# A layer norm and two matmuls on one core: the first three token tiles are transposed raw and corrected later

## The chip, the cores and the metric

The kernel runs on one core of one Trainium2 chip. The metric is the device time in microseconds of one launch. The core has five engines with instruction streams of their own, which wait for one another through semaphores: PE (TensorE, matmuls and transposes into PSUM), DVE (VectorE), ACT (ScalarE), POOL (GpSimd) and SP (SyncE, which here only issues DMA transfers).

## The reference

```python
def _layernorm(x, axis=-1, eps=1e-5):
    m = jnp.mean(x, axis=axis, keepdims=True)
    v = jnp.var(x, axis=axis, keepdims=True)
    return (x - m) / jnp.sqrt(v + eps)

# x (1, 2048, 1024), w1 (1024, 3584), b1 (3584), w2 (3584, 1024), b2 (1024), all bf16
def reference(x, w1, b1, w2, b2):
    y = _layernorm(x, axis=-1)
    h = _gelu(jnp.einsum("bsd,df->bsf", y, w1) + b1)     # tanh form
    return jnp.einsum("bsf,fd->bsd", h, w2) + b2
```

## The kernel before

The 2048 tokens are 16 tiles of 128, in four blocks of four tiles. The first matmul needs y with the contraction on the partitions, so each tile of x is normalised in its own layout and then transposed into `yT_sb` (two buffers, one block each, 8 contraction slices of 128). The first product runs over 28 rows (128 columns of w1 each). One row of one block is a PSUM bank: eight products of 128x128 weights with 512 columns. ACT evaluates GELU with b1 from PSUM into `hT_sb` (`act_gelu`, L430). The second product (`out_chunk`, L453) makes 128x512 pieces of the output with 28 products each; DVE adds b2 and SP stores them. PSUM has `ps_t` (one bank, for transposes at first and then a row), `ps_1` (five) and `ps_2` (two).

The program is written out as one list per engine, in order. Each operation names the events that it waits for and the event that it signals; `_emit` (L71) turns them into semaphore waits. An engine's order is therefore the order of the calls that built its list. Only DVE's list is partly planned: `crit` and `fill` are merged by estimated due times (L569 to L584).

The start is done differently from the rest. While the weights of the first seven rows arrive in eight chunks of one contraction slice each (`w0` to `w7`, 896 columns), block 0 is worked as a wave: 224 products of 128 columns for seven rows at a time, tile by tile and slice by slice (L505 to L534), into seven open banks. Transposes of block 0 are PE transposes (`pe_T`, L367) with a copy by ACT; from block 1 on, DVE transposes 32x32 blocks (`ops_T`, L344).

Tile 0 is centred with a mean that DVE and ACT take together (L274, L494), tile 1 with its mean alone (L286); their deviations are spread over the partitions later (`ops_rbc`, L326) and multiplied onto columns 0 to 255 of every row of block 0 in PSUM (`dve_scale`, L423). Tiles 2 and 3 are normalised in full before their transposes. The power -1/2 of the variance is POOL's (L268). Until the first tile is ready PE runs products of ones (`warm`, L488): 34, then 3, then 3.

After the wave, `mm1_rows` (L536) goes on with rows 7 to 27 of block 0, the first of them in bank `ps_t`, the next in the banks of rows 0 to 4 as their GELUs end.

Of the kernel before, what the change touches and what calls it, by code (L numbers as in the profile page):

```python
# [11 lines left out]
P = 128  # L12
# [3 lines left out]
K_GROUPS = 2  # L16
# [4 lines left out]
WARM_A = ((34, None), (3, "m4"))  # L21
WARM_B = 3
N_CENTRED = 2
T_PUTS = {0: (None, None, 6), 1: (21, 35), 2: (96, 118), 3: (140, 156)}
NORM = {0: (0, 2, 8), 1: (0, 4, 8), 2: (0, 4, 8)}
GROUPS_0 = (0, 2, 5, 8)
WAVE_ROWS_0 = 6
WAVE_K = (0, 2, 4, 5, 6, 8)
GROUPS_1 = (0, 4, 8)
W1_CHUNK_COLS = (512, 512, 1024, 640)  # L30
N_W2_CHUNKS = 4
SP_FIRST_LOADS = ("x0a", "w0", "w1", "w2", "w3", "w4", "w5", "x2a", "x2b", "w6", "w7", "x3a", "x3b", "b1", "w8")
ACT_FIRST_LOADS = ("x0b", "x1")

T_PE_START = 5.7
T_DVE_START = 16.5
# [54 lines left out]
def bass_standalone__mixer_channel_mlp__prompt_kernel(  # L91
# [22 lines left out]
    nkg = max(1, min(K_GROUPS, DT))  # L114
    KGROUPS = [(h * DT // nkg, (h + 1) * DT // nkg) for h in range(nkg)]
    assert NB1 + NB2 + 1 <= 8 and NB2 == 2
    assert all(c[-1] == DT for c in (*NORM.values(), GROUPS_0, GROUPS_1, WAVE_K))
# [27 lines left out]
    with ExitStack() as es:  # L145
# [19 lines left out]
        half_sb = sb("half_sb", [P, 1], F32)  # L165
        m4_sb = sb("m4_sb", [P, 1], F32)
        rq_sb = sb("rq_sb", [P, N_CENTRED, 32], F32)
        rbc_sb = sb("rbc_sb", [P, N_CENTRED, P], F32)

# [4 lines left out]
        ps_tf = ps_t[:, :, :].bitcast(F32)  # L174

# [37 lines left out]
        def issue(item):  # L213
            if item[0] == "x" and item[-1] in "ab":
# [44 lines left out]
        pool.op(lambda e: e.memset(b1r_sb[:, :], 0.0), sig="b1z")  # L259
        dve.op(lambda e: e.memset(st_sb[:, :, 12:14], 0.0))  # L260
# [6 lines left out]
        def op_aggr(i):  # L267
            pool.op(lambda e, i=i: e.tensor_tensor(out=rstd_sb[:, i:i + 1], in0=mv_sb[:, i, 1:2],  # L268
                                                   in1=nhalf[:, i:i + 1], op=ALU.pow),
                    waits=[f"mv{i}", "nhalf"], sig=f"rstd{i}")  # L270
            return (lambda e, i=i: e.bn_aggr(mv_sb[:, i, :], st_sb[:, i, :]),  # L271
                    [f"st{i}_0", f"st{i}_1", "eps"], f"mv{i}", 0.33)

        def op_mean0():  # L274
            return (lambda e: e.tensor_scalar(out=m4_sb[:, :], in0=st_sb[:, 0, 1:2], scalar1=st_sb[:, 0, 4:5],
                                              scalar2=half_sb[:, :], op0=ALU.add, op1=ALU.add),
                    ["st0_0", "half"], "m4", 0.1)

        def op_norm(i, c0, c1, sig):
            if i == 0:  # L280
                return (lambda e, c0=c0, c1=c1: e.tensor_scalar(
                            out=o_sb[:, 0, c0:c1], in0=x_sb[:, 0, c0:c1], scalar1=4.0,
                            scalar2=m4_sb[:, :], op0=ALU.mult, op1=ALU.subtract),
                        ["m4"], sig, 0.02 + (c1 - c0) * 0.00055)
            if i < N_CENTRED:
                return (lambda e, i=i, c0=c0, c1=c1: e.tensor_scalar(  # L286
                            out=x_sb[:, i, c0:c1], in0=x_sb[:, i, c0:c1], scalar1=mv_sb[:, i, 0:1],
                            scalar2=None, op0=ALU.subtract),
                        [f"mv{i}"], sig, 0.02 + (c1 - c0) * 0.00055)
            return (lambda e, i=i, c0=c0, c1=c1: e.tensor_scalar(  # L290
                        out=x_sb[:, i, c0:c1], in0=x_sb[:, i, c0:c1], scalar1=mv_sb[:, i, 0:1],
                        scalar2=rstd_sb[:, i:i + 1], op0=ALU.subtract, op1=ALU.mult),
                    [f"rstd{i}", f"mv{i}"], sig, 0.02 + (c1 - c0) * 0.00055)
# [3 lines left out]
        def ops_norm(i):  # L297
            cuts = NORM.get(i, (0, DT))
# [27 lines left out]
        def ops_rbc():  # L326
            res = []
            for i in range(N_CENTRED):
                res.append((lambda e, i=i: e.tensor_scalar(out=rq_sb[:, i, :], in0=ones[:, 0:32],
                                                           scalar1=rstd_sb[:, i:i + 1], scalar2=(1.0 if i else 0.25),  # L330
                                                           op0=ALU.mult, op1=ALU.mult),
                            ["ones", f"rstd{i}"], f"rq{i}", 0.1))
            for tq in range(4):
                for q in range(4):
                    src = rq_sb[32 * tq:32 * (tq + 1), :, :]
                    dst = rbc_sb[32 * q:32 * (q + 1), :, 32 * tq:32 * (tq + 1)]
                    res.append((lambda e, src=src, dst=dst: e.transpose(out=dst, in_=src), [f"rq{N_CENTRED - 1}"],  # L337
                                ("rbc" if tq == 3 and q == 3 else None), 0.1))
            return res
# [4 lines left out]
        def ops_T(i):  # L344
            blk, t = divmod(i, TPB)
            waits = [y_ev[i][-1]]
            if blk - 2 in mm1_done:
                waits.append(mm1_done[blk - 2])
            res = []
# [15 lines left out]
        t_banks = [("t", ps_t[:, 0, :]), ("2_0", ps_2b[:, 0, :]), ("t", ps_t[:, 0, :])]  # L365

        def pe_T(i, groups, k):  # L367
            blk, t = divmod(i, TPB)
            j0, j1 = groups[k], groups[k + 1]
            bname, bap = t_banks[k if i == 0 else 0]  # L370
            evs = yT_ev.setdefault(i, [None] * DT)
            for j in range(j0, j1):
                waits = []
                if j == j0:
                    waits = ["ident"] + ([bank_read[bname]] if bname in bank_read else [])
                if j == j0 or y_ev[i][j] != y_ev[i][j - 1]:
                    waits.append(y_ev[i][j])
                pe.op(lambda e, i=i, j=j, o=(j - j0) * P, bap=bap: e.transpose(  # L378
                    out=bap[:, o:o + P], in_=(x_sb[:, i] if i else o_sb[:, 0])[:, j * P:(j + 1) * P],
                    identity=ident[:, :]),  # L380
                    waits=waits, sig=(f"tp{i}_{k}" if j == j1 - 1 else None))
                evs[j] = f"te{i}_{k}"
            src = bap[:, 0:(j1 - j0) * P].rearrange("p (j s) -> p j s", j=j1 - j0)
            dst = yT_sb[:, blk % 2, j0:j1, t * P:(t + 1) * P]
            act.op(lambda e, dst=dst, src=src: e.copy(out=dst, in_=src), waits=[f"tp{i}_{k}"], sig=f"te{i}_{k}")  # L385
            bank_read[bname] = f"te{i}_{k}"
            pe_t[0] += (j1 - j0) * 0.056
# [20 lines left out]
        def pe_cell(b, r, t0, t1, bank, waits, sig, dts=None, opens=True, closes=True):  # L408
            n0, n1 = t0 * P, t1 * P
            dts = list(range(DT)) if dts is None else list(dts)  # L410
            waits = list(waits)
            for k, dt in enumerate(dts):
                w = (waits if k == 0 else []) + [f"w1c{w1_chunk_of(r, dt)}"]
                w += [yT_ev[b * TPB + t][dt] for t in range(t0, t1)]
# [213 lines left out]
```

## Time and profile before

| what | value |
|---|---|
| median of 3 runs | 398.43 us (398.41 to 398.49) |
| span of the profiled execution | 396.9 us; no other time is given for this execution |
| PE busy | 394.1 us, 99% of the span |
| DVE, ACT, POOL busy | 152.8, 82.8 and 9.7 us |
| instructions | 4883 |
| first wave, from its first product to the first product of row 7 | 5.92 to 20.16 us |
| DMA | 23.64 MB; 0.9 of the engines or more in the first five of 40 slices but the first (0.8) |

The profile is one execution, taken by the hardware profiler. Times in it are microseconds from the start of the span, "mean ns" is of one instruction, "L415" is a line of the kernel above, "PEld" is the loading of weights into PE, which runs beside its products, and "<-" names what ended an idle time. A chain of waits is followed back from the last instruction to what released it at each step; here it stays on PE nearly everywhere. PE's busy time is modelled for instructions that overlap, so the distance from one product to the next (216 ns at 512 columns) says more than the length of one (379 ns).

### The profile page before, as it was taken

How to read it: one execution, taken by the hardware profiler on the slowest of the kernel's cores; microseconds unless marked ns; L12 is line 12 of the kernel's file. 1: busy time of each engine (PE TensorE's matmuls, PEld its weight loads, DVE VectorE, ACT ScalarE, POOL GpSimd, SP SyncE). 2: the span in 40 equal slices, each digit the busy share in tenths (PEclk: the TensorE clock that was granted, in tenths of full speed). 3: DMA queues.
4: the chain of work that ended last, by engine and by line, in shares of the span. 5: the costliest groups of instructions: out<-in, count | busy, mean ns of one | idle time of the engine just before them, and what ended most of it. 6: DMA issues, size and time to landing. Idle time of an engine off the chain costs nothing.

```text
span 396.9 us, 4883 instructions
## 1 busy us (share of the span) xinstructions
PE 394.1 (99%) x2116; PEld 191.7 (48%) x2116; DVE 152.8 (38%) x345; ACT 82.8 (21%) x124; POOL 9.7 (2%) x24
## 2 busy tenths in 40 slices
PE   9999999999999999999999999999999999999998
PEld 8944444444444444444444444444444444444447
DVE  5847899989998005988100000001100000001011
ACT  4273430000133442000024433100003334400000
POOL 2101000020002000000000000000000000000000
PEclk9999999999999999999999999999999999999999
DMA  8999940000000000000000000000000000000000
GB/s 286 347 380 384 387 154 13 26 29 13 26 2 0 2 0 1 28 13 26 28 13 0 2 0 2 13 13 28 16 24 15 0 0 2 0 13 28 13 28 26
DMA packets 16924, 23.64 MB, mean 60 GB/s; under 512 B 1672, under 2 KB 10504, under 8 KB 16904
## 3 DMA queue, kind: packets, MB, share of 16 engines
q1 hardware_dynamic: 16616, 22.95, 16.4%
q8 instruction: 16, 0.26, 0.3%
q10 hardware_dynamic: 288, 0.39, 0.3%
q14 instruction: 4, 0.03, 0.0%
HBM read 19.14 MB, written 4.19 MB: 59 GB/s over the span
## 4 chain that ended last, share of the span: by engine, by line
PE 99%; ACT 0%; DVE 0%; issue 0%
PE ps L466 49%; PE ps L415 41%; PE ps_t L415 8%; PE ps L490 1%; PE ps_t L378 0%; ACT yT_sb L385 0%; DVE o_sb L477 0%
## 5 line engine op out<-in xcount | busy, mean ns | idle before, releaser
L466 PE MATMUL ps<-w_sb,hT_sb 128*128 128x512 bf16 (+1 forms) x980 | 194.2, 361 | 0.0
L415 PE MATMUL ps<-yT_sb,w_sb 128*128 128x512 bf16 (+1 forms) x920 | 167.4, 340 | 0.1
L466 PEld LDWEIGHTS ps<-w_sb,hT_sb 128*128 128x128 bf16 x980 | 91.3, 98 | 102.7
L415 PEld LDWEIGHTS ps<-yT_sb,w_sb 128*128 128x128 bf16 x920 | 80.9, 98 | 82.5 <-issue 0.3
L432 ACT ACTIVATE hT_sb<-ps,b_sb 128x512 bf16<-128x512 f32 x94 | 64.0, 688 | 237.2 <-PE ps L415 217.1
L477 DVE TENSOR_TENSOR o_sb<-ps,b_sb 128x512 bf16<-128x512 f32 (+1 forms) x35 | 22.6, 646 | 198.2 <-PE ps L466 198.1
L355 DVE STREAM_TRANSPOSE yT_sb<-x_sb 32x256 bf16<-32x256 bf16 x192 | 83.7, 436 | 26.6 <-PE ps_t L415 23.5
L415 PE MATMUL ps_t<-yT_sb,w_sb 128*128 128x512 bf16 x144 | 34.0, 379 | 0.0
L264 DVE BATCH_NORM_STATS2 st_sb<-x_sb 128x6 f32<-128x512 bf16 x32 | 21.1, 674 | 4.9 <-DMA x_sb<-in_x_dram 4.9
L415 PEld LDWEIGHTS ps_t<-yT_sb,w_sb 128*128 128x128 bf16 x144 | 14.0, 98 | 16.8
L432 ACT ACTIVATE hT_sb<-ps_t,b_sb 128x512 bf16<-128x512 f32 x18 | 12.4, 690 | 17.0 <-PE ps_t L415 14.6
L425 DVE TENSOR_TENSOR ps<-ps,rbc_sb 128x256 f32<-128x256 f32 x24 | 9.7, 426 | 6.1 <-PE ps L415 5.9
L268 POOL TENSOR_TENSOR rstd_sb<-mv_sb,nhalf 128x1 f32<-128x1 f32 x16 | 8.9, 559 | 118.7 <-DVE mv_sb L271 118.7
L290 DVE TENSOR_SCALAR x_sb<-x_sb,mv_sb,rstd_sb 128x1024 bf16<-128x1024 bf16 (+1 forms) x15 | 7.8, 525 | 3.9 <-POOL rstd_sb L268 3.3
L385 ACT COPY yT_sb<-ps_t 128x512 bf16<-128x512 bf16 (+2 forms) x8 | 4.4, 545 | 8.1 <-PE ps_t L378 8.1
L490 PE MATMUL ps<-const-bfloat16-1.0 128*128 128x128 bf16 x40 | 4.6, 302 | 0.8 <-PEq L613 0.8
L490 PEld LDWEIGHTS ps<-const-bfloat16-1.0 128*128 128x128 bf16 x40 | 4.0, 139 | 1.0 <-issue 0.8
L271 DVE BATCH_NORM_AGGREGATE mv_sb<-st_sb 128x2 f32<-128x15 f32 x16 | 3.5, 221 | 1.3
L337 DVE STREAM_TRANSPOSE rbc_sb<-rq_sb 32x64 f32<-32x64 f32 x16 | 3.8, 236 | 0.2
L378 PE MATMUL ps_t<-ident,x_sb 128*128 128x128 bf16 x24 | 2.3, 219 | 0.0
L425 DVE TENSOR_TENSOR ps_t<-ps_t,rbc_sb 128x256 f32<-128x256 f32 x4 | 1.6, 405 | 0.1
L493 ACT ACT_TABLE_LOAD x1 | 1.3, 1283 | 1.7 <-PEq L613 1.7
(24 smaller groups left out, 8.0 us busy)
## 6 DMA issues: line engine op xcount, KB each, us to landing
w_sb<-in_w_dram SPq DMA_DIRECT2D x4, 1792.0 KB, 18.3
out_dram<-o_sb SPq DMA_DIRECT2D x31, 128.0 KB, 1.7
x_sb<-in_x_dram SPq DMA_DIRECT2D x3, 1024.0 KB, 14.1
w_sb<-in_w_dram SPq DMA_DIRECT2D x2, 1024.0 KB, 9.1
w_sb<-in_w_dram SPq DMA_DIRECT2D x1, 2048.0 KB, 15.2
w_sb<-in_w_dram SPq DMA_DIRECT2D x8, 224.0 KB, 4.7
w_sb<-in_w_dram SPq DMA_DIRECT2D x1, 1280.0 KB, 14.7
x_sb<-in_x_dram SPq DMA_DIRECT2D x5, 128.0 KB, 4.6
```

Source lines behind the costliest of these rows:

```text
L264: return (lambda e, i=i, h=h: e.bn_stats(st_sb[:, i, 6 * h:6 * (h + 1)], x_sb[:, i, h * HC:(h + 1) * HC]), [x_ev[i][h]], f"st{i}_{h}", 0.65)
L268: pool.op(lambda e, i=i: e.tensor_tensor(out=rstd_sb[:, i:i + 1], in0=mv_sb[:, i, 1:2], in1=nhalf[:, i:i + 1], op=ALU.pow), waits=[f"mv{i} ...
L290: return (lambda e, i=i, c0=c0, c1=c1: e.tensor_scalar(out=x_sb[:, i, c0:c1], in0=x_sb[:, i, c0:c1], scalar1=mv_sb[:, i, 0:1], scalar2=rst ...
L337: res.append((lambda e, src=src, dst=dst: e.transpose(out=dst, in_=src), [f"rq{N_CENTRED - 1}"], ("rbc" if tq == 3 and q == 3 else None), ...
L355: res.append((lambda e, src=src, dst=dst: e.transpose(out=dst, in_=src), waits, (f"tr{i}" if lastop else None), 0.47))
L385: act.op(lambda e, dst=dst, src=src: e.copy(out=dst, in_=src), waits=[f"tp{i}_{k}"], sig=f"te{i}_{k}")
L415: pe.op(lambda e, b=b, r=r, dt=dt, n0=n0, n1=n1, bank=bank: e.matmul(unit_bank(bank)[:, n0:n1], lhsT=w1_sb[:, dt, r * P:(r + 1) * P], rhs= ...
L425: crit.append((est[wait_ev], (lambda e, ap=ap: e.tensor_tensor(out=ap, in0=ap, in1=rbc_sb[:, :, :].rearrange("p t s -> p (t s)"), op=ALU.m ...
L432: act.op(lambda e, r=r, n0=n0, n1=n1, bank=bank: e.activation(out=hT_sb[:, r, n0:n1], in_=unit_bank(bank)[:, n0:n1], func=ACT.Gelu_apprx_tanh,
L466: pe.op(lambda e, st=st, ft=ft, c0=c0, c1=c1, bank=bank: e.matmul(ps_2[:, bank, 0:c1 - c0], lhsT=hT_sb[:, ft, st * P:(st + 1) * P], rhs=w2 ...
L477: crit.append((est[sig], (lambda e, ob=ob, c0=c0, c1=c1, bank=bank: e.tensor_tensor(out=o_sb[:, ob, c0:c1], in0=ps_2[:, bank, 0:c1 - c0], ...
L490: pe.op(lambda e: e.matmul(ps_1[:, 0, 0:P], lhsT=unit, rhs=unit, start=True, stop=True), waits=[gate] if gate else [])
```

## The change

Tiles 0 to 2 of block 0 are no longer normalised before the first wave. They are loaded in halves of the contraction (three first halves, then the three second halves as one transfer, `xrb`), transposed raw into the second buffer of `yT_sb`, which block 1 uses later, and multiplied raw. A column of ones behind the three tiles, column 384, makes the sum of every weight column in the same products; ACT copies it out (`act_cs`). For rows 0 to 6 DVE applies deviation and mean in PSUM afterwards (`ops_corr`): multiply by a row of deviations, add the weight sum times a row of minus mean times deviation.

These two rows are made so: statistics on DVE, the power for three tiles at once on POOL (`rstdr`), the product on DVE (`op_nmr`), four transposes on DVE (`ops_rvt`), and two broadcasts over the partitions on POOL (`row0`, `row1`). For rows 7 to 27 the raw tiles are corrected once, from the second buffer of `yT_sb` into the first (`ops_fix`): tile 0 and half of tile 2 on DVE, tile 1 and the other half of tile 2 on POOL. The four closing events are `FX`. Row 7 starts with tile 3, which is normalised as before, and then takes tiles 0 to 2. Block 1's transposes wait for `FX` as well. Dummy products are 24, in one go.

The core of the diff (`...` where lines are left out):

```diff
-WARM_A = ((34, None), (3, "m4"))
-WARM_B = 3
-N_CENTRED = 2
...
+WARM = 24
+N_RAW = 3
+RC = N_RAW * P
+HALVES = (0, 4, 8)
-SP_FIRST_LOADS = ("x0a", "w0", "w1", "w2", "w3", "w4", "w5", "x2a", "x2b", "w6", "w7", "x3a", "x3b", "b1", "w8")
-ACT_FIRST_LOADS = ("x0b", "x1")
+SP_FIRST_LOADS = ("x0a", "w0", "w1", "xrb", "w2", "w3", "w4", "x3a", "x3b", "w5", "w6", "w7", "b1", "w8")
+ACT_FIRST_LOADS = ("x1a", "x2a")
...
+        def op_nmr():
+            return (lambda e: e.scalar_tensor_tensor(out=rv_sb[:, N_RAW:2 * N_RAW, 0], in0=mv_sb[:, 0:N_RAW, 0],
+                                                     scalar=-1.0, in1=rv_sb[:, 0:N_RAW, 0], op0=ALU.mult,
+                                                     op1=ALU.mult),
+                    ["rstdr"] + [f"mv{i}" for i in range(N_RAW)], "nmr", 0.15)
+        def ops_rvt():
+            return [(lambda e, q=q: e.transpose(out=rvt_sb[:, :, 32 * q:32 * (q + 1)],
+                                                in_=rv_sb[32 * q:32 * (q + 1), :, :]),
+                     ["nmr"], ("rvt" if q == 3 else None), 0.37) for q in range(4)]
...
+        def ops_fix(i, tmp, j0, j1, tag, prev):
+            s0, s1 = i * P, (i + 1) * P
+            bc = lambda k: row_sb[:, k:k + 1, s0:s1].to_broadcast([P, j1 - j0, P])
+            return [(lambda e: e.tensor_tensor(out=tmp[:, 0:j1 - j0, :], in0=yT_sb[:, 1, j0:j1, s0:s1], in1=bc(0),
+                                               op=ALU.mult),
+                     ["row0", f"te{i}_0", f"te{i}_1"] + prev, f"fm{i}{tag}", 1.2),
+                    (lambda e: e.tensor_tensor(out=yT_sb[:, 0, j0:j1, s0:s1], in0=tmp[:, 0:j1 - j0, :], in1=bc(1),
+                                               op=ALU.add),
+                     [f"fm{i}{tag}", "row1"], f"fx{i}{tag}", 1.2)]
...
         def ops_T(i):
...
+            elif blk == 1:
+                waits += [f"cw_{R - 1}"] + list(FX)
...
+        def y_waits(b, t0, t1, dt):
+            if b == 0:
+                return [f for f in FX if t0 <= int(f[2]) < t1] + [yT_ev[i][dt] for i in range(max(t0, N_RAW), t1)]
+            return [yT_ev[b * TPB + t][dt] for t in range(t0, t1)]
...
+        raw = list(range(N_RAW))
+        head = [op_stats(i, h) for h in range(2) for i in raw] + [op_aggr(i) for i in raw]
+        pool.op(lambda e: e.tensor_tensor(out=rv_sb[:, 0:N_RAW, 0], in0=mv_sb[:, 0:N_RAW, 1], in1=nhalf[:, 0:N_RAW],
+                                          op=ALU.pow),
+                waits=[f"mv{i}" for i in raw] + ["nhalf", "rv0"], sig="rstdr")
+        head += [op_stats(N_RAW, 0), op_stats(N_RAW, 1), op_aggr(N_RAW), op_nmr()] + ops_rvt() + ops_norm(N_RAW)
...
+        for k in range(2):
+            pool.op(lambda e, k=k: e.partition_broadcast(
+                row_sb[:, k, 0:RC], rvt_sb[0:1, k * N_RAW:(k + 1) * N_RAW, :].rearrange("p v s -> p (v s)")),
+                waits=["rvt", "row1c"], sig=f"row{k}")
+        head += ops_b1()
+        h = DT // 2
+        FX = ["fx0v", "fx1p", "fx2v", "fx2p"]
+        head += ops_fix(0, tmp_sb, 0, DT, "v", []) + ops_fix(2, tmp_sb, 0, h, "v", ["fx0v"])
+        for fn, waits, sig, _ in ops_fix(1, tmp2_sb, 0, DT, "p", []) + ops_fix(2, tmp2_sb, h, DT, "p", ["fx1p"]):
+            pool.op(fn, waits=waits, sig=sig)
+        for o in head:
             dve_put(o)
...
+        def ops_corr(r):
+            ap = unit_bank(wave[r][0])[:, 0:RC + 1]
+            return [(lambda e: e.tensor_tensor(out=ap, in0=ap, in1=row_sb[:, 0, :], op=ALU.mult),
+                     [f"m1_0_{r}", "row0", "row1c"], f"sa_{r}", 0.55),
+                    (lambda e: e.scalar_tensor_tensor(out=ap, in0=row_sb[:, 1, :], scalar=cs_ap[r], in1=ap,
+                                                      op0=ALU.mult, op1=ALU.add),
+                     [f"sa_{r}", cs_ev[r], "row1"], f"sb_{r}", 0.62)]
...
+        first, most, every = range(NB1), [*range(NB1), R - 1], range(R)
+        pe_T([(0, 0)], "t")
+        pe_T([(1, 0)], "2_0")
+        cells(first, (0,), 0, 1)
+        pe_T([(2, 0)], "2_1")
+        cells(first, (0,), 1, 2)
+        cells((R - 1,), (0,), 0, 2)
+        cells(most, (1,), 0, 2)
+        cells((NB1,), (0, 1), 0, 2)
+        pe_T([(0, 1), (1, 1)], "t")
+        cells(every, (0, 1), 2, 3)
+        cells(every, (2,), 0, 3)
+        pe_T([(2, 1)], "t")
+        cells(every, range(3, DT - 1), 0, 3)
+        pe_T([(3, 0)], "t")
+        cells(first, (DT - 1,), 0, 3)
+        act_cs(ps_1, 0, NB1, False)
+        cells(range(NB1, R), (DT - 1,), 0, 3)
+        act_cs(ps_2, NB1, R, True)
+        pe_T([(3, 1)], "t")
+        r4 = R // 2 + 1
+        late_cells(3, range(r4), range(h))
+        late_cells(3, range(r4), range(h, DT))
+        late_cells(3, range(r4, R), range(DT))
+        for o in corr:
+            dve_put(o)
         def mm1_rows(b, r0):
             for r in range(r0, FT):
-                mm1_row(b, r)
+                mm1_row(b, r, ((N_RAW, TPB), (0, N_RAW)) if b == 0 and r == r0 else ((0, TPB),))
```

`cells(rows, slices, t0, t1)` issues the wave's products on raw tiles t0 to t1 - 1, one for all of them together (128 columns a tile, and column 384 where tile 2 is among them); `late_cells` does tile 3.

## The prediction

> **What bounds the kernel now.** I read the page first (busy shares, the chain that ended last), then the chain in order of time for the first 60 us, then POOL and DVE in order of time, then the groups by shape.
>
> ```profile
> PE 394.1 (99%) x2116; PEld 191.7 (48%) x2116; DVE 152.8 (38%) x345; ACT 82.8 (21%) x124; POOL 9.7 (2%) x24
> PE 99%; ACT 0%; DVE 0%; issue 0%
> ```
>
> PE is never without work, and the chain lies on it. A matmul removed, or PE beginning useful work earlier, shortens the run by as much; a wait of PE lengthens it by as much. The chain in order of time (start, length, what) shows where useful work begins:
>
> ```profile
> 0.82 4.26 PE ps L490 x37
> ...
> 5.40 0.38 ACT yT_sb L385
> 5.78 0.14 issue
> 5.92 0.49 PE ps L415 x6
> ...
> 16.37 3.80 PE ps L415 x68
> 20.16 1.73 PE ps_t L415 x8
> ```
>
> Dummy products until 5.08, the first real product at 5.92, the first wave (rows 0 to 6) until 20.16, then row 7. From there on PE runs 216 ns products without a gap to 395.10. So only the 20.16 us to the start of row 7 and the readiness of row 7's operands are in play. The other engines' price rows, from the order in time (start, length) and from the groups by shape:
>
> ```profile
> 0.78 0.20 POOL L254 MEMSET ones<- 128x128 bf16 x1 [0.29 <-POOLq L613]
> 1.05 0.29 POOL L255 TENSOR_SCALAR_AFFINE_SELECT ident<-ones 128x128 bf16<-128x128 bf16 x1
> ...
> 6.73 0.62 DVE L286 TENSOR_SCALAR x_sb<-x_sb,mv_sb 128x512 bf16<-128x512 bf16 x2
> 6.78 0.72 POOL L268 TENSOR_TENSOR rstd_sb<-mv_sb,nhalf 128x1 f32<-128x1 f32 x1 [5.32 <-DVE mv_sb L271]
> ...
> 8.29 0.55 POOL L268 TENSOR_TENSOR rstd_sb<-mv_sb,nhalf 128x1 f32<-128x1 f32 x1 [0.78 <-DVE mv_sb L271]
> ```
>
> ```profile
> L425 DVE TENSOR_TENSOR ps<-ps,rbc_sb 128x256 f32<-128x256 f32 x18 | 7.1, 424 | 6.0 <-PE ps L415 5.9
> L337 DVE STREAM_TRANSPOSE rbc_sb<-rq_sb 32x64 f32<-32x64 f32 x16 | 3.8, 236 | 0.2
> L385 ACT COPY yT_sb<-ps_t 128x512 bf16<-128x512 bf16 x6 | 3.5, 585 | 6.4 <-PE ps_t L378 6.4
> L493 ACT ACT_TABLE_LOAD x1 | 1.3, 1283 | 1.7 <-PEq L613 1.7
> ```
>
> POOL has done only short work so far: single-column powers, and nothing wider than 128 elements.
>
> **The gain at the start.** The 24 dummy products run at 107 ns (34 of them took 3.54 us on PEld) from 0.82 to 3.39. The first half tile is there at 3.25, where DVE's first statistics begin. Four transposes at 107 ns end at 3.82, their copy takes 0.585, and the hand-over seen above 0.14: first product at about 4.57 instead of 5.92. From there I count the new order with the row's 55.9 ns for 128 columns (68 in 3.80), which with 215.8 ns for 512 (8 in 1.73) gives 109 for 256 and 163 for 385. 10 of 128 columns 0.56; 9 of 256, 0.98; 14 of 129, 0.79; 42 of 385, 6.85; 56 of tile 3, 3.13; 24 transposes 1.33: 13.64 us, against 14.24 before. Rows at the start (6 products in 0.49, not 0.34) say that hand-overs add some 0.3. Row 7 then begins at 18.5 instead of 20.16: 1.65 us won, less 0.02 because row 7 comes in two pieces. I take 1.6, with 1.0 to 2.0 as bounds.
>
> The removed work on ACT and DVE (mean 0.63 and 0.27, centring, 16 small transposes 3.98, 28 scalings of 0.42) lay beside PE; only the first centring stood on its path, and the step from 5.92 to 4.57 holds it. The loads moved on SP's and ACT's queues are early enough: from 5 to 7.5 us the trace moved 345 GB/s, 1.03 MB being in by 5 us, so the 1.25 MB through "xrb" land at 5.6. The same count puts the second tile of before at 8.2, where it came at 8.9; I add the 0.7 and have "xrb" at 6.3 and tile 3 at 9.0. PE wants the second halves at about 6.6. Weight chunks follow faster (229 KB, 0.65 us) than PE uses one (7 x 163 ns = 1.14 us).
>
> **The new wait.** Row 7's second piece reads tiles 0 to 2 of yT's other buffer, and waits for all four FX events. Behind that matmul stands the whole rest of PE's program. PE reaches it at 18.5 + 8 x 0.056 = 18.95. When do the events come? DVE: three second-half statistics (0.64 each, as two took 1.28) from 6.3 to 8.2, three aggregations of 0.22 to 8.85, tile 3's statistics and aggregation from 9.0 to 10.5, the product for the mean 0.2, four transposes of 32x192 (between the 0.236 of 32x64 and the 0.436 of the 32x256 bf16 row; 0.37 each): 12.2. POOL meanwhile ends tile 3's power at 11.15.
>
> Then POOL writes two rows of 384 elements to all partitions. No row of the trace has this. By the memset (0.10 for one column, 0.204 for 128: 0.8 ns an element) it is 0.4 us, by twice the one-input select (1.5 ns an element) 1.3; I take 0.7 each. POOL then multiplies and adds 3072 elements per partition in four instructions with two inputs each: at 0.8 ns 2.9 us, at twice the select's 1.5 ns 9.6; the select's rate half as much again, 2.25 ns, gives 7.3, which I take. DVE's four halves are cheap: 0.16 + 1.04 ns an element (by the 256-wide row) sums to 3.7. A kind of instruction that POOL has not run may first have to fetch its code, and the trace prices no such thing, so bounds: nothing; 1.28 us (the table load of ACT, on idle queues); 4.6 us (the median landing of an x transfer issued in the first 20 us, when the DMA engines are full, share 1.0 to 1.06); 6.4 us (the same for the weights in the first 30 us). Longer ones (up to 20) waited behind megabytes on their own queue, which is no case for a separate fetch. POOL's place in time is the full stretch, so I take 4.6, twice: on going to the broadcasts, and on coming back to products.
>
> Sum: first load 11.15 + 4.6 = 15.75; two rows, 17.15; second load, 21.75; four products, 29.05. PE stands from 18.95 to 29.05: 10.1 us. After such a stand I expect the dummy products' pace again: at the start some 37 ran at 107 instead of 56 ns, 1.9 us lost (bounds 0 and 1.9; the granted clock reads 1.0 throughout and does not show it). Total 10.1 - 1.6 + 1.9 = +10.4.
>
> The Trainium skill ("GPSIMD Engine Reference", Instruction dispatch) says that the first call after a Pool library is loaded pays about 6 us for it, with no instruction in the profile; no run here shows that yet. By an estimate from the 5.95 us that the Trainium skill gives there, twice, the sum would be about +13.
>
> Queued behind the waits: on DVE the correction pairs of rows 0 to 6 stand behind its own FX work; 14 of 0.56 us (385 wide, 0.426 + 129 x 1.04 ns) from 20.2 on end at 28, and their GELUs free the banks for rows 8 and later before PE asks. Without a stall the first pair starts at 17.1, its GELU ends at 19.0, and row 8 wants the bank at 20.2: the cover is 1.2 us. Block 1's transposes wait for FX too, but began at 42.6 before. POOL's later powers and SP's loads stand behind nothing new that matters.
>
> **The time.** The profiled execution has a span of 396.9 us and no time of its own beside it; the runs' median 398.43 lies 1.53 above the span, and I carry that over: 398.4 + 10.4 = 408.8. On the bounds for a load: at 1.28 the products end at 22.4, PE stands 3.4 us, +1.8, 400.2; at 6.4 they end at 32.65, +14.0, 412.4.
>
> **Rivals.** (a) One load serves both kinds: rows at 17.15, products at 24.45, PE stands 5.5, 404.2; if POOL and DVE also exclude each other, DVE's 3.7 and POOL's 7.3 run in series from 16.45 to 27.45, 407.2. Chance 0.15. For it: no row says that one load cannot hold both kinds; against: none says that it can, and the powers ran before any broadcast.
> (b) No load shows, and the two engines' products exclude each other: 12.9 + 11.0 = 23.9, PE stands 4.95, less 1.6, plus half the slow restart: 402.7. Chance 0.22. For it: the power beside DVE's centring took 0.72, the one with DVE idle 0.55. The Trainium skill ("SBUF — State Buffer", Who interferes with whom) says that a VectorE instruction with two SBUF inputs and a GpSimd one that reads SBUF exclude each other for their whole length; the 0.72 agrees in kind, though that was a one-tensor form. In the forecast DVE finishes (20.2) while POOL is still loading, so it costs nothing there.
> (c) No load, no exclusion, POOL at 2.25 ns: 13.6 + 7.3 = 20.9, a stand of 1.95, +0.3, 398.7. Chance 0.05.
> (d) The other side: no load, and POOL at the memset's 0.8 ns. Products end at 13.0 + 2.9 = 15.9, before 18.95, and the 1.6 us stay: 396.8. It decides where POOL's work after the transposes (12.2) fits into 6.75 us. For it: POOL is 2% busy, and 3072 elements are little; against: its only one-input row is twice as slow, and its single-column power costs 0.55. Chance 0.13.
>
> **How the numbers follow.** The forecast has 0.45. What a measurement can tell from no change is about 0.2%, 0.8 us. Slower: forecast, (a) and (b), 0.82; same: (c), 0.05; faster: (d), 0.13. The range 400 to 413 holds all slower cases with the bounds of the load, and leaves out (c), (d) and a little above, 0.2.
>
> **What would show it.** Right: PE's first L415-like product at 4.4 to 4.8, row 7 reached near 18.5; POOL gaps of several us ahead of the first broadcast and of the first wide product; POOL's last product near 29; in the chain, POOL's line ahead of PE's row 7, and products at about 107 ns spacing behind it. Wrong: FX events by 19 us (then faster), gaps of POOL that are not there (then b or c), PE waiting for "xrb" or weights before 18 us, or a wave that starts later than 5.

## The result and the profile after

The changed kernel takes 418.50 us in the median of four runs (418.19 to 419.48), the kernel before, on the same chip, 398.42 us (398.27 to 398.49): a ratio of 1.0509, with a 95% interval of 1.0494 to 1.0524, or 20.1 us more. The profiled execution has a span of 417.5 us, 20.6 more than the 396.9 before.

The page of the changed kernel first: PE's row of busy time, the granted clock in 40 slices, and the chain that ended last.

```profile
PE 394.7 (95%) x2015; PEld 188.5 (45%) x2015; DVE 149.3 (36%) x316; ACT 83.1 (20%) x123; POOL 16.6 (4%) x31
PEclk9955999999999999999999999999999999999999
PE 94%; issue 4%; POOL 2%; ACT 0%; DVE 0%; POOLq 0%; ACTq 0%
```

PE is busy for as long as before (394.7 us against 394.1), but in a longer span. The chain has gained 4% of "issue" and 2% of POOL, and the granted clock falls to half in the third and fourth slice. The chain in order of time (start, length, what) shows where:

```profile
4.78 0.67 PE ps L413 x5
...
16.46 5.10 issue
21.56 1.23 POOL row_sb L503 x2
...
22.86 9.56 issue
...
39.24 2.72 PE ps_t L413 x8
41.96 9.12 PE ps L413 x40
```

The wave starts at 4.78 instead of 5.92. Then the chain leaves PE for POOL: two stretches in which POOL waits for nothing that the profile shows, each before another kind of POOL instruction. POOL in order of time (start, length, instruction, idle time before it and its cause):

```profile
10.73 0.56 POOL L272 TENSOR_TENSOR rstd_sb<-mv_sb,nhalf 128x1 f32<-128x1 f32 x1 [0.58 <-DVE rv_sb L279]
21.56 1.23 POOL L503 PARTITION_BROADCAST row_sb<-rvt_sb  x2 [10.27 <-issue]
32.42 2.13 POOL L334 TENSOR_TENSOR tmp_sb<-yT_sb,row_sb 128x1024 f32<-128x1024 bf16 x1 [9.63 <-issue]
34.63 2.00 POOL L337 TENSOR_TENSOR yT_sb<-tmp_sb,row_sb 128x1024 bf16<-128x1024 f32 x1
...
38.01 1.09 POOL L337 TENSOR_TENSOR yT_sb<-tmp_sb,row_sb 128x512 bf16<-128x512 f32 x1
```

DVE's last transpose of the two rows ended at 12.22, so the broadcasts had their operands 9.3 us before they ran; the first product had its own from 22.79 on, and 9.63 us later began. Between two instructions of one kind there is no such gap. Broadcasts themselves took 1.23 us for two, the four products 6.7 from 32.42 to 39.11. PE in order of time:

```profile
18.80 0.61 PE L413 MATMUL ps_t<-yT_sb,w_sb 128*128 128x128 bf16 x8
39.24 2.72 PE L413 MATMUL ps_t<-yT_sb,w_sb 128*128 128x384 bf16 x8 [19.84 <-POOL yT_sb L337]
```

The same view of the kernel before has row 7 here:

```profile
20.00 1.89 PE L415 MATMUL ps_t<-yT_sb,w_sb 128*128 128x512 bf16 x8
```

So row 7 is reached at 18.80 instead of 20.00, 1.20 us earlier. (The 20.16 of the chain before counts from the end of the wave's last product; counted so, the changed kernel reaches row 7 at 18.96.) Its second piece starts 20 us later, behind POOL's last sum. The windows of the changed kernel (stretch, its length, busy time of PE, PEld, DVE, ACT and POOL, granted clock, DMA share, GB/s) show the clock in that stand and after it:

```profile
25.00:30.00 5.00, 0.00 (x0) 0.00 (x0) 4.77 (x9) 1.44 (x3) 0.00 (x0) 0.50 1.06 384
40.00:45.00 5.00, 5.00 (x20) 2.16 (x18) 4.56 (x10) 1.38 (x2) 1.10 (x2) 0.72 1.05 388
```

From 45 us on the clock is at 1.00 again. The account: 1.20 earlier at row 7; its first piece, 0.45; a stand, in which PE does nothing, of 19.84; its second piece 2.72, where row 7 before took 1.73 as a whole; and the next 40 products 9.12 instead of 8.63. That is -1.20 + 0.45 + 19.84 + 2.72 - 1.73 + 0.49 = 20.57, against 20.6 in the spans.

### The profile page after: what moved, and what is told of

Read it like the earlier page. It is cut to its first block, busy times and chain, and to the rows that moved or that the text cites. A ratio compares the mean times of both kernels' runs of the same rounds, so it can differ in the third digit from the quotient of the medians.

```text
span 417.5 us, 4668 instructions
## 1 busy us (share of the span) xinstructions
PE 394.7 (95%) x2015; PEld 188.5 (45%) x2015; DVE 149.3 (36%) x316; ACT 83.1 (20%) x123; POOL 16.6 (4%) x31
## 4 chain that ended last, share of the span: by engine, by line
PE 94%; issue 4%; POOL 2%; ACT 0%; DVE 0%; POOLq 0%; ACTq 0%
PE ps L465 46%; PE ps L413 38%; PE ps_t L413 8%; POOL tmp_sb L334 1%; POOL yT_sb L337 1%; PE ps L489 1%; PE ps_t L381 0%; POOL row_sb L503 0%; ACT yT_sb L389 0%; DVE o_sb L476 0%; PE ps L381 0%; ACT cs_sb L534 0%; POOLq L334 0%; POOLq L72 0%; ACTq L72 0%
## 5 line engine op out<-in xcount | busy, mean ns | idle before, releaser
L413 PE MATMUL ps<-yT_sb,w_sb 128*128 128x512 bf16 (+4 forms) x827 | 167.5, 361 | 0.3 <-ACT yT_sb L389 0.3
L413 PEld LDWEIGHTS ps<-yT_sb,w_sb 128*128 128x128 bf16 x827 | 77.8, 98 | 85.6 <-issue 1.1
L413 PE MATMUL ps_t<-yT_sb,w_sb 128*128 128x512 bf16 (+2 forms) x152 | 35.4, 378 | 19.8 <-POOL yT_sb L337 19.8
L290 DVE TENSOR_SCALAR x_sb<-x_sb,mv_sb,rstd_sb 128x1024 bf16<-128x1024 bf16 x13 | 7.1, 546 | 6.0 <-POOL rstd_sb L272 5.2
L334 DVE TENSOR_TENSOR o_sb<-yT_sb,row_sb 128x1024 f32<-128x1024 bf16 (+1 forms) x2 | 2.1, 1074 | 9.2 <-POOL row_sb L503 9.1
L389 ACT COPY yT_sb<-ps_t 128x512 bf16<-128x512 bf16 x6 | 3.4, 587 | 7.7 <-PE ps_t L381 7.7
L545 DVE SCALAR_TENSOR_TENSOR ps<-row_sb,cs_sb,ps 128x385 f32<-128x385 f32 x7 | 4.4, 623 | 0.2
L543 DVE TENSOR_TENSOR ps<-ps,row_sb 128x385 f32<-128x385 f32 x7 | 3.9, 560 | 0.0
L334 POOL TENSOR_TENSOR tmp_sb<-yT_sb,row_sb 128x1024 f32<-128x1024 bf16 (+1 forms) x2 | 3.3, 1642 | 9.8 <-issue 9.6
L337 POOL TENSOR_TENSOR yT_sb<-tmp_sb,row_sb 128x1024 bf16<-128x1024 f32 (+1 forms) x2 | 3.1, 1545 | 0.2
## 6 DMA issues: line engine op xcount, KB each, us to landing
w_sb<-in_w_dram SPq DMA_DIRECT2D x1, 2048.0 KB, 14.4
```

The costliest lines, as they stand in the source:

```text
L290: return (lambda e, i=i, c0=c0, c1=c1: e.tensor_scalar(out=x_sb[:, i, c0:c1], in0=x_sb[:, i, c0:c1], scalar1=mv_sb[:, i, 0:1], scalar2=rst ...
L334: return [(lambda e: e.tensor_tensor(out=tmp[:, 0:j1 - j0, :], in0=yT_sb[:, 1, j0:j1, s0:s1], in1=bc(0), op=ALU.mult), ["row0", f"te{i}_0" ...
L337: (lambda e: e.tensor_tensor(out=yT_sb[:, 0, j0:j1, s0:s1], in0=tmp[:, 0:j1 - j0, :], in1=bc(1), op=ALU.add), [f"fm{i}{tag}", "row1"], f"f ...
L413: pe.op(lambda e: e.matmul(unit_bank(bank)[:, n0:n1], lhsT=w1_sb[:, dt, r * P:(r + 1) * P], rhs=yT_sb[:, buf, dt, n0:n1], start=start, sto ...
L545: (lambda e: e.scalar_tensor_tensor(out=ap, in0=row_sb[:, 1, :], scalar=cs_ap[r], in1=ap, op0=ALU.mult, op1=ALU.add), [f"sa_{r}", cs_ev[r] ...
```

## The experiments

The program as built holds an instruction that changes POOL's set of code ahead of the broadcasts (and of their wait for the rows, so it is reached at 11.29, when the last power ends), and another ahead of the products; in the kernel before there is one only, ahead of the select that makes the identity. The theory: POOL holds code for one set of instruction kinds at a time, and going over from powers and products to broadcasts, and back, each fetches code for 8 to 10 us. Rivals: the broadcast itself, a wait that the profile does not show, or POOL and DVE excluding each other. In all of the following the kernel before, on the same chip, took 398.4 us.

**The price of a fetch by itself.** In the kernel before, POOL runs two broadcasts and then two products on a tile of its own that nobody reads: once behind tile 3's power, while the weights stream in, and once behind the last power.

```diff
+            if i in (TPB - 1, NT - 1):
...
+                for n in range(2):
+                    pool.op(lambda e: e.partition_broadcast(db_sb[:, 0:384], da_sb[0:1, 0:384]), ...)
...
+                for n in range(2):
+                    pool.op(lambda e: e.tensor_tensor(out=db_sb[:, :], in0=da_sb[:, :], in1=da_sb[:, :], op=ALU.mult), ...)
```

> The kernel before, with idle work added on POOL at two places: after the power of tile 3 (about 14 us, DMA engines full until about 45 us) and after the power of the last tile (beyond 140 us, DMA nearly idle): two broadcasts of 384 elements, then two products of 1024 elements, on a scratch tile. Theory 1 (each change of kind makes POOL fetch code, and the fetch shares the DMA engines): about 10 us of gap before the first broadcast and before the first product at the early place, about 5 to 6 us at the late one, and none between the two of a kind. Theory 2 (the fetch has a fixed length): 10 us at both places. Rival (a broadcast or a wide product is slow to start by itself): a gap before each of the two of a kind too. The time stays within 0.3 us of the kernel before, since nothing waits for this work but the powers of block 1, 50 us ahead of their use.

It took 398.36 us in one run: nothing waits for these. POOL in order of time:

```profile
22.68 1.44 POOL L277 PARTITION_BROADCAST db_sb<-da_sb  x2 [8.46 <-issue]
32.30 3.85 POOL L280 TENSOR_TENSOR db_sb<-da_sb 128x1024 f32<-128x1024 f32 x2 [8.18 <-issue]
...
135.03 1.44 POOL L277 PARTITION_BROADCAST db_sb<-da_sb  x2 [5.77 <-issue]
143.40 3.85 POOL L280 TENSOR_TENSOR db_sb<-da_sb 128x1024 f32<-128x1024 f32 x2 [6.93 <-issue]
```

A change of kind costs a gap in both directions, with no operand to wait for, and the second instruction of a kind has none. The size goes with the traffic: 8.46 and 8.18 us where the DMA share is 1.05 to 1.07, 5.77 and 6.93 where it is 0.00 to 0.01.

**The same price in the changed kernel with quiet DMA engines.** Here the weight loads from the tenth on wait for POOL's last sum; nothing else is changed.

```diff
-                load_w1(ci)
+                load_w1(ci, ["fx2p"] if ci == DT + 1 else [])
```

> The changed kernel, with the weight loads from the tenth on held back until POOL's last product, so that the DMA engines have nothing to move from some 12.5 us on until then. Theory (POOL's code comes through the DMA engines and is slowed by the loads: 5.8 to 6.9 us with idle engines and 8.2 to 10.5 with busy ones): the two gaps of POOL shrink from 10.3 and 9.6 us to about 6 to 7 each, the last product ends near 32 instead of 39, and the time is 411 to 412 us, or some more where a later row of weights is then late. Rival (the length of a fetch depends on where POOL comes from or what it fetches, not on the traffic): gaps of 10.3 and 9.6 as before, last product at 39, 418 us or more.

It took 412.28 us, 6.2 less than the changed kernel, although its weights come later. POOL, and the windows inside the two gaps:

```profile
17.75 1.23 POOL L503 PARTITION_BROADCAST row_sb<-rvt_sb  x2 [6.04 <-issue]
25.96 2.12 POOL L334 TENSOR_TENSOR tmp_sb<-yT_sb,row_sb 128x1024 f32<-128x1024 bf16 x1 [6.98 <-issue]
```

```profile
11.80:17.70 5.90, 5.90 (x65) 4.43 (x63) 1.66 (x6) 1.50 (x4) 0.00 (x0) 1.00 0.32 108
19.00:25.90 6.90, 0.60 (x11) 0.43 (x8) 6.62 (x10) 1.37 (x2) 0.00 (x0) 0.75 0.00 0
```

The gaps fell from 10.27 and 9.63 to 6.04 and 6.98, by 6.9 us together, and the last sum came at 32.64 instead of 39.11. So some 60 and 70% of the two gaps belong to the fetch itself, and the rest to the weights that stream in beside it. By which way the code comes is not shown: in the second gap of this run the trace has no DMA packet at all. Nor is it settled why the gaps under full DMA engines were 8.2 to 8.5 us in the run before this and 9.6 to 10.3 in the changed kernel.

**One change of kind less.** All correction of tiles 0 to 2 goes to DVE; POOL only broadcasts.

```diff
-        FX = ["fx0v", "fx1p", "fx2v", "fx2p"]
...
+        FX = ["fx0v", "fx1v", "fx2v"]
+        head += ops_fix(0, tmp_sb, 0, DT, "v", []) + ops_fix(1, tmp2_sb, 0, DT, "v", [])
+        head += ops_fix(2, tmp_sb, 0, DT, "v", ["fx0v"])
```

> The changed kernel with all of the correction of tiles 0 to 2 on DVE; POOL only broadcasts. The first gap stays and the second is on nobody's path. Theory: rows at 21.6 to 22.8, six DVE products of about 1.2 us from 22.2 end at 29.7, PE stands 10.4 us from 19.25, about 409.5 us (9 less than the change). Rival (DVE's products were the slow part): no gain.

409.67 us (ratio 1.0282, 1.0262 to 1.0303). The gap before the broadcasts stayed (10.49 us), DVE's six operations ran from 22.49 to 30.00, five of them at 1.22 to 1.23 us and the first at 1.46, and PE stood until 30.14. POOL's next power, at 39.50, had no gap ahead of it but its wait for DVE's statistics: the way back was fetched while nothing waited for it. The second fetch and POOL's products together had held PE for 9.1 us more (39.24 against 30.14).

**The slow restart.** 340 products of ones stand ahead of row 7, so that PE is busy while it waits.

```diff
+        for n in range(N_FILL):
+            pe.op(lambda e: e.matmul(ps_tf[:, 0, 0:P], lhsT=unit, rhs=unit, start=True, stop=True), ...)
```

> The changed kernel with 340 dummy products of 128 columns on PE ahead of row 7, into row 7's bank, which fill PE's stand almost to its end (340 x 0.056 = 19 us). Theory (part of the loss is PE's slower clock after the stand, worked out from the spacings as 1.9 us): granted clock 1.0 throughout, row 7's second piece in 1.3 instead of 2.7 us, about 416.6 us. Rival (the spacing after the stand has another cause, such as POOL and PE both reading): no change, 418.5.

417.08 us, 1.4 less than the changed kernel, with POOL's gaps at 10.70 and 8.82 us and the granted clock at 1.0 throughout. PE in order of time:

```profile
38.96 1.91 PE L414 MATMUL ps_t<-yT_sb,w_sb 128*128 128x128 bf16 x16
```

Row 7 now ran its 16 products from 38.96 to 40.71, and the rows behind it at 216 ns. In the changed kernel the eight products of the second piece took 2.72 us, where behind a short stand, which slows nothing, they take 1.46 (a run below shows it), and the next 40 took 9.12 instead of 8.63: 1.75 us lost. The fill wins this back, less 0.45 for row 7's first piece, which now lies behind the stand; POOL's last sum, 0.16 us earlier here, adds the rest. So the slow products come from PE's standing idle.

**No change of kind at all, by one set of code for both.** Behind its first memsets POOL loads a set that holds the broadcast and the products.

```diff
+        pool.op(lambda e: e.load_library(library_config.all_libraries[10]))
```

> The changed kernel with one code set named for POOL by hand, right after its first memsets (1.7 us), that holds both the broadcast and the products, so that POOL need not change later. Theory (the two gaps are code fetches): both gaps of 10.3 and 9.6 us vanish; a fetch of 10 us from 1.7 holds up the first power to about 12 instead of 9.3, rows at 15.9, POOL's products end at 22.6, PE stands 3.4 us: about 400.5 us. With a fetch of 6 us rows at 13.6, products at 20.3, PE stands 1.1: 398.2. If DVE's and POOL's products exclude each other, up to 4 us more. Rival (the gaps belong to the instructions themselves): gaps as before, 418 us or more.

406.54 us (1.0205, 1.0188 to 1.0222). Both gaps are gone: the broadcasts follow the rows, and the products the broadcasts. But a new one had come at the very start, as POOL in order of time shows:

```profile
9.76 0.28 POOL L255 TENSOR_SCALAR_AFFINE_SELECT ident<-ones 128x128 bf16<-128x128 bf16 x1 [8.77 <-DVE mv_sb L277]
...
18.08 1.54 POOL L505 PARTITION_BROADCAST row_sb<-rvt_sb  x2 [1.35 <-DVE rvt_sb L287]
19.48 3.08 POOL L336 TENSOR_TENSOR tmp_sb<-yT_sb,row_sb 128x1024 f32<-128x1024 bf16 x1
```

The page puts it down to DVE, but the select reads nothing of DVE's, and came at 1.29 in the changed kernel. It makes the identity for the PE transposes, and the first of these ran at 10.10, so the wave began at 11.39 instead of 4.78. (The named set itself then kept POOL idle for 5.03 us ahead of its first power, which began at 15.30.) The likely cause of the late select: the launch before had left the other set in POOL. Two runs test that. One takes the kernel before and adds one broadcast of 16 elements as POOL's last instruction, far behind its last use; the other takes the kernel with one load and adds a select as POOL's last instruction, which brings the first set back.

```diff
+        pool.op(lambda e: e.partition_broadcast(db_sb[:, :], nhalf[0:1, :]), waits=["nhalf"])
```

> The kernel before with a single broadcast of 16 elements to a scratch tile at the end of POOL's program (beyond 140 us, nothing waits for it). Theory (the code set left behind is paid for by the next launch): the first select comes some 8 us late, the first PE transpose, which needs its result, at about 9.8 instead of 5.0, and the run takes 402 to 405 us. Rival: 398.4 us, as nothing on the path has changed.

POOL in order of time, at the start of this launch:

```profile
10.14 0.28 POOL L256 TENSOR_SCALAR_AFFINE_SELECT ident<-ones 128x128 bf16<-128x128 bf16 x1 [9.15 <-issue]
```

The otherwise untouched kernel took 405.52 us (1.018, 1.0161 to 1.0199). The broadcast itself came at 141.75 behind a gap of 5.80 and delayed nothing; what it cost was the next launch's first select, at 10.14 instead of 1.05.

```diff
+        pool.op(lambda e: e.load_library(library_config.all_libraries[10]))
...
+        pool.op(lambda e: e.affine_select(out=end_sb[:, :], in_=ones[:, :], ...))
```

> The kernel of e2_oneload with one select more at the very end of POOL's program, written to a scratch tile, whose only effect is that POOL ends with the first code set again. In e2 the first select of the launch came at 9.76 us instead of 1.29. Theory (a launch that finds another code set in POOL pays for the first one again): the first select is back at 1.3, the fetch of the combined set runs from 1.8 for 5 to 9 us, rows of deviations at 13.4 to 15, and POOL's and DVE's products, which slow each other down, end 9.5 later at 22.3 to 24.5; PE stands 3 to 5 us; 400 to 403 us. Rival (the late select has another cause, such as the named code set itself): the select stays at 9.8 and the time at 406.5.

403.86 us (1.0134, 1.0119 to 1.0148). The select is back at 1.28, which confirms the cause; the set is fetched while POOL waits for DVE's statistics, and the rows are out by 14.4. Still PE stood 3.63 us, since the corrections had become slow. POOL's and DVE's in order of time:

```profile
14.28 3.08 POOL L337 TENSOR_TENSOR tmp_sb<-yT_sb,row_sb 128x1024 f32<-128x1024 bf16 x1
17.43 2.86 POOL L340 TENSOR_TENSOR yT_sb<-tmp_sb,row_sb 128x1024 bf16<-128x1024 f32 x1
```

```profile
15.39 3.05 DVE L340 TENSOR_TENSOR yT_sb<-o_sb,row_sb 128x1024 bf16<-128x1024 f32 x1
18.54 2.30 DVE L337 TENSOR_TENSOR o_sb<-yT_sb,row_sb 128x512 f32<-128x512 bf16 x1
```

The same instructions took 2.13 and 2.00 on POOL and 1.23 and 0.69 on DVE in the changed kernel, where they did not meet. Their ends here alternate: POOL 17.36, DVE 18.44 (1.08 later), POOL 20.29 (1.85 later), DVE 20.84 (0.55 later). Each ends its own length, less some 0.15, after the other's end, as if one ran while the other stood. This agrees with the Trainium skill ("SBUF — State Buffer", Who interferes with whom), by which a VectorE instruction with two inputs in SBUF and a GpSimd one that reads SBUF exclude each other.

**Whether POOL's help is worth it.** As the last kernel, but all float32 correction on DVE.

```diff
-        FX = ["fx0v", "fx1p", "fx2v", "fx2p"]
...
+        FX = ["fx0v", "fx1v", "fx2v"]
```

> The changed kernel with one set of code for both kinds, the first set put back at the end, and all of the correction of the three tiles (six float32 operations of 128x1024 and 128x512) on DVE; POOL keeps the power and the broadcasts. Theory (POOL and DVE hold each other up when both work on float32 tiles at once: 3.08 and 2.86 us for POOL's products and 3.05 and 2.31 us for DVE's in the run with POOL's help, 1.23 us for DVE alone): rows at about 13.9 us, then DVE alone at about 1.23 us per operation, done near 21.3, PE stands some 2 us instead of 3.6, and the whole takes 400.5 to 401.5 us, 2 to 3 less than with POOL's help (403.9). Rival (the long products were slow for another reason, such as the rows being read by many partitions): DVE's products keep 2.3 to 3 us each, the correction ends at 27 or later, and the time is above 405.

399.95 us (1.0039, 1.0026 to 1.0053), 3.9 less than with POOL's help. DVE and PE in order of time:

```profile
15.15 1.23 DVE L340 TENSOR_TENSOR yT_sb<-o_sb,row_sb 128x1024 bf16<-128x1024 f32 x1
```

```profile
21.32 1.46 PE L416 MATMUL ps_t<-yT_sb,w_sb 128*128 128x384 bf16 x8 [1.68 <-DVE yT_sb L340]
```

Six operations, five of them at 1.22 to 1.23 us, from 13.65 to 21.16 beat two engines that take turns until 23.36. After a stand of 1.68 us the second piece was not slow (1.46); after 3.63 us it was (2.72).

**The rows without any broadcast.** 16 DVE transposes of 32x192 write both rows to all partitions; products stay on both engines.

```diff
+            res = [(lambda e: e.tensor_copy(rq_sb[:, :, :], rv_sb[:, :, 0:1].to_broadcast([P, 2 * N_RAW, 32])), ...)]
+            for tq in range(4):
+                for q in range(4):
...
+                    res.append((lambda e, src=src, dst=dst: e.transpose(out=dst, in_=src), ["rq"], ...))
```

> The changed kernel with the two rows made on DVE alone, by sixteen small transposes as the kernel before does it, and no broadcast on POOL; POOL keeps its half of the correction. Theory: no code is fetched; rows at 10.7 + 0.3 + 16 x 0.37 = 17, then POOL's and DVE's products, slowing each other, 9.5 us, to 26.5; PE stands 7.2 us; 398.4 - 1.4 + 7.2 and up to 1.9 for the slow restart: 404 to 406 us, 12 to 14 less than the change. Rival (POOL's wide products bring a gap of their own): 410 us or more.

405.66 us (1.0184, 1.0165 to 1.0202). POOL had no gap: rows at 17.28, products from 17.36. But the loss lay elsewhere than the theory had it, and the time fell into the expected range by luck. DVE's normalisation of tile 3 stood behind the 6.14 us of transposes:

```profile
17.32 2.46 DVE L297 TENSOR_SCALAR x_sb<-x_sb,mv_sb,rstd_sb 128x1024 bf16<-128x1024 bf16 x1
```

It took 2.46 us instead of 0.55, beside POOL's first product (17.36 to 19.49). PE waited 5.47 us for it in the middle of the wave and ran the rest of the wave slowly (56 products in 4.58 us instead of 3.29); at row 7 it had no stand at all.

**A version without the price.** First, rows converted to bfloat16 by POOL, and the correction on DVE in bfloat16, with the load of one set and the select at the end:

```diff
+        pool.op(lambda e: e.load_library(library_config.all_libraries[10]))
...
+        pool.op(lambda e: e.tensor_copy(rowb_sb[:, :, :], row_sb[:, :, 0:RC]), waits=["row0", "row1"], sig="rowb")
+        head += ops_fix(0, tmb_sb, 0, DT, "v", []) + ops_fix(1, tmb2_sb, 0, DT, "v", [])
+        head += ops_fix(2, tmb_sb, 0, DT, "v", ["fx0v"])
```

> As e5_restore, with the two rows also copied to bf16 by POOL, and all of the correction of tiles 0 to 2 on DVE with bf16 operands throughout (six products of 1024 elements). Theory: with no code to fetch in the way, rows at 13.4, copies at 14.4, six DVE products of some 0.65 us (a bf16 form may run two elements a cycle; if not, 1.2 us) end at 18.2 (or 21.8), before PE wants them at 19.25 (or 2.5 late); corrections of rows 0 to 6 follow in time for row 8. So 397.1 us, 1.3 less than the kernel before (or 399.6). Rival (the early start itself loses what it gains, in later stages): 398.4 or more though PE does not stand.

397.68 us (0.9983, 0.9974 to 0.9992): less than both kernels, though only 0.7 us less than the kernel before (eleven runs from 397.43 to 398.10, against 398.05 to 398.51). The six operations take 0.69 us each and end at 19.4, and PE stands 0.23 us at row 7 and 0.53 at row 8. The power still began 1.1 us after its operands (10.00 against 8.90), most likely because the set was still being fetched. The last kernel makes the identity by an iota on POOL and a comparison on DVE, so that one set of code serves the whole launch and the next, and converts each row right behind its broadcast (the first four DVE operations also alternate between tiles 0 and 1):

```diff
-        pool.op(lambda e: e.affine_select(out=ident[:, :], in_=ones[:, :], pattern=[[-1, P]],
...
+        pool.op(lambda e: e.load_library(library_config.all_libraries[10]))
+        pool.op(lambda e: e.iota(io_sb[:, :], pattern=[[-1, P]], base=0, channel_multiplier=1), sig="io")
+        dve.op(lambda e: e.tensor_scalar(out=ident[:, :], in0=io_sb[:, :], scalar1=0.0, scalar2=None, op0=ALU.is_equal), ...)
```

> One load, the rows cast to bfloat16 on POOL, the correction on DVE in bfloat16, as in the run of 397.68 us; but the identity is made by an iota and a comparison on DVE, so that only the set of code that the broadcasts use is ever needed, and the next launch finds it. Theory (a fetch is paid only where the set in POOL is another one, also from launch to launch): no gap on POOL in the whole launch, the power at about 9.0 us instead of 10.0, the rows about 1 us earlier, no stand of PE before row 7, and 396.8 to 397.4 us. Rival (each launch fetches once in any case, or the iota needs the first set): the identity comes 6 to 9 us late and the time is near 405.

397.23 us (0.9969, 0.9957 to 0.9981). The interval overlaps the one above, so these two are not told apart, but both are below the kernel before. The chain and POOL in order of time:

```profile
2.09 5.00 DMA x_sb<-in_x_dram
...
19.20 1.75 PE ps_t L417 x16
```

```profile
9.52 0.88 POOL L500 TENSOR_TENSOR rv_sb<-mv_sb,nhalf 128x3 f32<-128x3 f32 x1 [8.06 <-DVE mv_sb L279]
...
12.55 0.67 POOL L507 PARTITION_BROADCAST row_sb<-rvt_sb  x1 [1.04 <-DVE rvt_sb L289]
```

POOL has no gap that lacks a cause, its power follows the statistics (9.28) by 0.24 us, and row 7 runs its 16 products without a stand. The power did not come at 9.0 as expected, since the second halves of x landed later than in the changed kernel (DVE's statistics of them began at 7.11 instead of 6.87). PE waited 0.53 us for them too, and began their transposes at 7.13 instead of 6.89. That is the whole 0.24 us by which the chain has row 7 later than in the changed kernel (19.20, not 18.96). Tile 3's normalisation took 1.02 us instead of 0.55 beside the first broadcast, but ended at 13.51, and PE's transposes of tile 3, from 14.32 on, did not wait for it. Of the 1.6 us that the prediction gave to the start, this version keeps 1.1 (398.37 to 397.23).

## Why the prediction was right or wrong

The mechanism and its place were right: a stand of PE at row 7's second piece, made by two code fetches on POOL and the products behind them. The size was not, and the time fell above the range.

| term | predicted | measured |
|---|---|---|
| first product of the wave | 4.57 | 4.78 |
| row 7 reached (counted as in the chain) | 18.5 | 18.96 |
| second halves of x there | 6.3 | 6.87 |
| POOL's last power before the broadcasts ends | 11.15 | 11.29 |
| rows transposed by DVE | 12.2 | 12.22 |
| fetch before the broadcasts | 4.6 | 10.27 |
| two broadcasts | 1.4 | 1.23 |
| fetch before the products | 4.6 | 9.63 |
| POOL's four products | 7.3 | 6.7 |
| stand of PE | 10.1 | 19.84 |
| slow restart | 1.9 | 1.75 |

**The step that failed** is the term of the fetch, which was too small, twice. It was priced by the median landing of an x transfer under full engines, 4.6 us, with 6.4 as upper end, and the longer landings "up to 20" were put aside because they waited behind their own queue. The nearest row, ACT's table load, and the transfers were all other things than this; and the table load, taken as one on idle queues, had run at a DMA share of 0.89. The runs show 5.8 to 7.1 us on quiet engines and 8.2 to 10.7 on busy ones. Of the 10.7 us by which the two gaps of the changed kernel (19.9) exceed the 9.2 taken, 3.8 remain with the weights held back (6.04 and 6.98), and 6.9 come with the weights that stream in beside. With 10.27 and 9.63 in place of 4.6 and 4.6 the prediction's own sum gives +21.1, within one microsecond of the 20.1 measured; the products, 0.6 shorter than taken, make most of the rest.

Smaller slips of the sum cost nothing here. By its own rate DVE's four operations come to 3.83 us, not 3.7; they took 4.24 and were done long before POOL's. The lower end of 400.2 has no slow restart in it, though a stand of 3.63 us brought one (2.72 us for the eight products); with 1.9 it would be 402.1. And the rows were ready at 12.22 as forecast partly by luck: the second halves of x came 0.57 us late, while the three aggregations took 0.37 us instead of 0.66.

The sentence on the Trainium skill ("GPSIMD Engine Reference", Instruction dispatch) came nearer, +13 by twice its 5.95 us. The trace agrees with it where the DMA engines are quiet (5.77, 5.80, 6.04, and 6.68 to 7.14 on the way back) and exceeds it by 2 to 5 us where the weights stream in, which is where this change puts both fetches.

**The rivals.** (a) One load for both kinds: not so as the program stands; where it was made so, both gaps went. (b) Exclusion is real, as the run with one set and POOL's help shows: corrections in series until 23.36, against the 23.9 that the rival had. That is near by luck: they began at 13.89 instead of 12.9 and took 9.5 us instead of 11.0. In the change it costs nothing, as the forecast said: DVE's four operations end at 26.51, and POOL's first begins at 32.42. (c) and (d) fell with the gaps; POOL's rate of 2.1 ns an element, near the 2.25 taken, alone would have ruled out (d), whose 2.9 us of products were 6.7.

**What hid and what did not.** The corrections of rows 0 to 6 on DVE took 0.56 and 0.62 us and ended at 34.4, before row 7's second piece: covered, but only by the stand. In the kernel with bfloat16 rows, where row 7's stand has shrunk to 0.23 us, row 8 waited 0.53 us for its bank's GELU, the cover of 1.2 us that the prediction named being used up. The prediction had the slow restart nearly right in size (1.9 against 1.75). It noted that the granted clock reads 1.0 at the start, where products are slow as well; behind the stand the clock does show it, 0.50 in the stand and 0.72 behind it.

## What to carry to other kernels

Count the changes of instruction kind on POOL as you would count DMA round trips: each was 6 to 7 us with quiet DMA engines and 8 to 11 with busy ones, and the profile shows it only as an idle time put down to "issue" (or to an engine from which the instruction reads nothing). Look also at which kind POOL ends the launch with, since the next launch pays for it at its start. And before giving POOL half of a float32 product of two SBUF tiles, check whether DVE is at the same: here DVE alone was done 2 us sooner than both.

## What the runs showed of the hardware that was not expected

- A set of code left in POOL by one launch costs the next its first select: 9.76 and 10.14 us instead of 1.05 to 1.29.
- The fetch is slowed by other loads: 5.8 to 7.1 us at a DMA share of 0.33 or less, 8.2 to 10.7 at 1.05 or more. The set for both kinds took 5.03 us at a share of 0.55, in the kernel with one load (POOL idle from 10.27 to 15.30).
- POOL's 1024-element product of two tiles and DVE's lengthen each other to 3.08 and 3.05 us, from 2.13 and 1.23. Operations of DVE with one tensor input can be held up too: beside POOL's products the normalisation took 2.46 us instead of 0.55, and the conversion of b1 behind it 1.74 instead of 0.18. DVE's corrections in PSUM, with one input from SBUF, were not: 0.56 and 0.62 us before and beside POOL's first product in the changed kernel.
- DVE's product of 1024 elements takes 0.69 us where both inputs and the output are bfloat16, and 1.23 where one of them is float32.
- PE's first 384-column products after a stand of 3.63, 10.72, 13.18 or 19.84 us run at about half pace (2.72 us for eight), and after one of 1.68 or 1.73 us they do not (1.46).
